# Attention products of two key tiles in one run of every second filled step, ten exponential buffers, eight GLU row buffers

## The chip, the cores and the metric

One core of one Trainium2 chip. The metric is device time in microseconds of one execution: the kernel before took 2319.98 us, the median of three runs (2316.81 to 2325.04).

## The reference

Two layers, each an attention block and a GLU block, over 2048 rows of 448 numbers. Both blocks normalise their input (layer norm without weights) and add their result to it. Both layers use the same weights.

```python
q = (x @ wq)   # 16 heads of 28
k = x @ wk     # one head, shared by all 16
v = x @ wv
p = softmax(q k^T * 28 ** -0.5)
x = x + (p v) @ wo
h = sigmoid(x @ w_gate) * (x @ w_up)     # 1792 columns
x = x + h @ w_down
```

## The kernel before

The schedule is written by hand: the order in which the Python code issues instructions is the order of each engine's queue. Each projection uses fp16 operands split into a high and a low part.

Attention runs per layer in 256 steps (lines 1100 to 1131): 16 query tiles `u` of 128 rows, and in each 16 key tiles `kt` of 128 keys. A string, `ORDER`, lists what a step issues, letter by letter:

- `S`: `scores` (line 598). One matmul of a key tile with the queries of four heads into a bank `s`, then ScalarE's exponential into a tile `P` of 128 x 512 (L604). Four per step, one for each group of four heads.
- `P`: `pv` (line 607), the attention product of the step before: four fp32 matmuls (L612), each of 32 columns of the array, side by side, accumulated over the 16 key tiles in the bank `pv`. Each is issued as two instructions, so a product is eight instructions: two passes of four. After the last key tile ScalarE copies the bank to `pvs` (L616).
- `M`: one part of the row maxima of a later query tile (`mx_gen`, line 570): four matmuls `mx`, each on 32 rows of the array, side by side, in four banks (L584), and four VectorE reductions of them (L588). The generator is ahead of the scores and runs out before the layer's steps do.
- `F`: `fill.slice` (line 936), a slice of queued matmuls of other work: the GLU of earlier row blocks (`gp`, `up` through `chain`, L402; `dn`, L802), the output projection (`wo`, L705), the next layer's queries. The slice's size follows from the work left and the steps left (`rate`), shared over the `F` of a step. It also issues what was deferred for the other engines.
- `X`: bookkeeping of the side work (`tick`), loads and preparation.

`s`, `mx` and all fill banks come from one ring of seven banks (tag `f`, `NBK`); a bank is taken again when its reader is done. `pv` has an eighth bank of its own. The tiles `P` come from a ring of eight buffers (tag `P`, line 603), which at the start also holds four input tiles and an index tile (lines 80, 81).

GLU work of a layer begins when its first block of two row tiles is ready (`BLK[l, 0].fed == TB`). `ORDERS` (line 1084) has one string for the steps before and one for those after, both the same here; the choice is made at the start of a step, before `X` in which a block becomes ready. I call steps after it filled. A GLU block makes seven tiles `h` of 128 x 2 x 512 in fp16 (line 769), then its down products read them. `h` has `HB` = 9 buffers. At the start the same buffers stage 42 pieces of the weights (line 248), whose squares are summed on TensorE (L144) to find scales. The start is ordered by a small list scheduler (`Plan`, line 868) with assumed costs; `HB` limits how many pieces it loads ahead (line 1073).

```python
1084  ORDERS = ["XFSFSFSFSPM", "XFSFSFSFSPM"]
1103  ORDER = ORDERS[(l, 0) in BLK and BLK[l, 0].fed == TB]
1110  elif o == "P":
1111      if prevP is not None:
1112          pv(*prevP)
1130  fill.slice(rate / ORDER.count("F"))
1131  prevP = (l, u, kt, P)
```

Of the kernel before, what the change touches and what calls it, by code (L numbers as in the profile page):

```python
# [8 lines left out]
F32 = mybir.dt.float32  # L9
F16 = mybir.dt.float16  # L10
BF16 = mybir.dt.bfloat16
I32 = mybir.dt.int32
# [8 lines left out]
def interleaved_layers_kernel(ctx: ExitStack, tc: tile.TileContext, x, wq, wk, wv, wo, wg, wu, wd, out, layers=2):  # L21
# [7 lines left out]
    _, S, D = x.shape  # L29
# [1 line left out]
    H, Dh = 16, 28  # L31
    NT, NB, G, KT, FC = S // 128, S // 512, H // 4, S // 128, F // 128
    U = NT
    TB, WB, HB, PF = 2, 4, 9, [4]
    NBL = NT // TB
    RQE, LD = nc.scalar, (0, 1, 2, 3)
    X0, X1, X2, X3, X4 = 3.0, 0.75, 5.0, 11.0, 17.0
# [10 lines left out]
    wk1 = ctx.enter_context(tc.tile_pool(name="wk1", bufs=2))  # L48
# [14 lines left out]
    xr0 = {}  # L63

    def load_x0(i, n, buf, eng=nc.sync):
        v = buf.rearrange("p n -> p () n") if n == 1 else buf
        eng.dma_start(v, x[0, i * 128:(i + n) * 128].rearrange("(t p) n -> p t n", p=128))
        for t in range(n):
            xr0[i + t] = v[:, t]
# [7 lines left out]
    load_x0(8, 2, wk1.tile([128, 2, D], F32, tag="XT2", name="xr0"))  # L77
    load_x0(10, 2, wk1.tile([128, 2, D], F32, tag="XT2", name="xr0"))
    for i in range(12, NT):
        load_x0(i, 1, wk1.tile([128, D], F32, tag="P", name="xr0", bufs=8))  # L80
    jp = wk1.tile([128, 128], I32, tag="P", name="jp", bufs=8)
    nc.gpsimd.iota(jp, pattern=[[1, 128]], base=0, channel_multiplier=-1)
    id16 = cst.tile([128, 128], F16, name="id16")
    nc.vector.tensor_scalar(id16, jp, 0.0, None, op0=OP.is_equal)
# [21 lines left out]
    def flush(every=False):  # L106
        todo, pend[:] = pend[:], []
        for i, (due, fn) in enumerate(todo):
            if due > now[0] and not every:
                pend.append((due, fn))  # L110
            else:
                fn()
        if every and pend:
            flush(True)
# [219 lines left out]
    def paced(step):  # L334

        k = next((i for i in range(len(PLAN) - 1) if PLAN[i + 1][0] > step), None)
        if k is None:
            n = 10 ** 6
        else:
            (a, p), (b, q) = PLAN[k], PLAN[k + 1]  # L340
            n = p + (q - p) * (step + 1 - a) / (b - a)
        while prepd[0] < n and ready[0] < 2 + FC:
            next(prep[0])
            prepd[0] += 1
# [76 lines left out]
    def layer_tiles(l):  # L421
        KK[l] = lay.tile([128, 2, S], F16, tag="KK", name="KK")
        VV[l] = lay.tile([128, KT, 32], F32, tag="VV", name="VV")
        nc.vector.memset(VV[l][:, :, 28:32], 0.0)
        nc.vector.memset(VV[l][:, :, 28:29], 1.0)
# [93 lines left out]
    def parts_of(l, u):  # L519

        ends = KEYS[l > 0 and u == 0]
        return list(zip(ends, ends[1:]))
# [11 lines left out]
    def load_qh(l, u):  # L534
        b, t = divmod(u, 4)
        if l + b == 0:
            QH[l, u] = QH0[:, :, t * 128:(t + 1) * 128]
            return
        assert QDONE[l, b] == G
        q = wk1.tile([128, G, 128], F16, name="QH", bufs=2)  # L540
        QH[l, u] = q
        nc.sync.dma_start(q, qd[l % 2][b, :, 0, :, t * 128:(t + 1) * 128].rearrange("g p n -> p g n"))
# [6 lines left out]
    def mx_ready(l, n):  # L549

        keys = parts_of(l, 0)
        return KVD[l] * 128 >= keys[n // G][1] if n < G * len(keys) else True
# [45 lines left out]
    def scores(l, u, kt, g, P):  # L598
        assert ("m", l, u) in stored, (l, u, kt)
        s = psf.tile([128, 512], F32, tag=BANKS["s"], name="s", bufs=NBK[BANKS["s"]])  # L600
        nc.tensor.matmul(s, KK[l][0:96, 0, kt * 128:(kt + 1) * 128], QS[l, u][:, g].rearrange("p h n -> p (h n)"),  # L601
                         start=True, stop=True)
        p = wk1.tile([128, 512], F32, tag="P", name="P", bufs=8)
        nc.scalar.activation(p, s, AF.Exp, scale=esc)  # L604
        P.append(p)

    def pv(l, u, kt, P):
        if kt == 0:
            PVS[l, u] = psv.tile([128, 512], F32, tag="v", name="pv")
        v = PVS[l, u]  # L610
        for g in range(4):
            nc.tensor.matmul(v[32 * g:32 * g + 32], VV[l][:, kt], P[g], start=kt == 0, stop=kt == KT - 1,  # L612
                             tile_position=(0, 32 * g))
        if kt == KT - 1:
            o = wk1.tile([128, 512], F32, name="pvs", bufs=1)
            nc.scalar.copy(o, v)  # L616
            PVS[l, u] = o


    XTQ, BLK = {}, {}  # L620
    side, held = [], set()

    def later(*stages):

        side.append([stages[0][0], list(stages)])

    def tick():

        for s in list(side):
            s[0] -= 1  # L630
            if s[1][0][1].__name__ in ("fd", "db") and held:
                s[0] = max(s[0], 1)
            if s[0] <= 0:
                flush()
                fill.run(s[1].pop(0)[1]())
                if s[1]:
                    s[0] = s[1][0][0]
                else:
                    side.remove(s)
# [441 lines left out]
    xr0 = None  # L1081

    early[0] = False
    ORDERS = ["XFSFSFSFSPM", "XFSFSFSFSPM"]
    MORE = (5, 10)
    FIRST = KT * TB + 16
    KEEP = 28000
# [1 line left out]
    for l in range(layers):  # L1089
        mx = mxs[l]  # L1090
        final = l + 1 == layers
        if not final:
            layer_tiles(l + 1)
        fill.slice(QCH)
        flush(True)
        next(mx, None)
        fill.slice(QCH)
        prevP = None
        rate = 0.0
        for step in range(U * KT):  # L1100
            u, kt = divmod(step, KT)
            P = []
            ORDER = ORDERS[(l, 0) in BLK and BLK[l, 0].fed == TB]
            for o in ORDER:
                if o == "S":
                    scores(l, u, kt, len(P), P)
                elif o == "M":
                    for _ in range(1 + (u == 0 and kt in MORE)):
                        next(mx, None)
                elif o == "P":  # L1110
                    if prevP is not None:
                        pv(*prevP)
                elif o == "X":
                    if u == U - 1 and not final and (l + 1, 0) not in QH and QDONE.get((l + 1, 0)) == G:
                        load_qh(l + 1, 0)
                    if u and kt == 1:
                        b = (u - 1) // TB
                        if (l, b) not in BLK:
                            BLK[l, b] = Block(l, b)
                        later(*BLK[l, b].tile(u - 1))  # L1120
                    if l == 0:
                        paced(step)
                    tick()
                    fed = sum(BLK[l, b].fed == TB for b in range(NBL) if (l, b) in BLK)
                    if fed < NBL - 1:
                        rate = fill.left / max(FIRST + TB * KT * fed - step, 1)
                    else:
                        rate = max(fill.left - KEEP, 0) / (U * KT - step)
                else:
                    fill.slice(rate / ORDER.count("F"))  # L1130
            prevP = (l, u, kt, P)
        pv(*prevP)
        flush(True)
        later(*BLK[l, NBL - 1].tile(U - 1))
        if not final:
            mxs[l + 1] = mx_gen(l + 1)
        n = done = 0
        last = G * len(parts_of(l + 1, 0))
        while side or pend or fill.urgent or (fill.gens if final else done < last):
            tick()  # L1140
            for _ in range(4):
                fill.slice(VS / 4)
            n += 1
            if not final and done < last and QDONE.get((l + 1, 0)) == G and mx_ready(l + 1, done):
                if n >= 3 or done >= last - G:
                    next(mxs[l + 1])
                    done += 1
                    n = 0
# [21 lines left out]
```

## Time and profile before

| | us |
|---|---|
| median of three runs | 2319.98 |
| profiled execution, own time | 2324.69 |
| its span, first to last instruction | 2322.9 |
| TensorE matmul busy | 2239.4 |
| VectorE busy | 1633.2 |
| ScalarE busy | 1549.8 |

The granted TensorE clock averages 0.99 of full speed. Times in rows are microseconds from the span's start unless marked ns; PE is TensorE, PEld its weight loads, DVE VectorE, ACT ScalarE. `out<-in` are the program's names, x is the number of instructions merged in a row. The end of a matmul is modelled and includes its way through the array, so successive matmuls overlap in a row's times; the distance from one start to the next is what TensorE spent. In square brackets stands how long the engine sat idle before, and what released it.

### The profile page before, as it was taken

What the parts mean: (1) busy time and instruction counts of PE and PEld (TensorE: products, weight loads), DVE (VectorE), ACT (ScalarE), POOL (GpSimd) and SP (SyncE); (2) the same over time, 40 slices, a digit from 0 to 9 for tenths busy, and PEclk for the clock granted to TensorE, in tenths of its full rate; (3) what the DMA queues carried; (4) which work ended last, traced back from release to release, by engine and by line L of the source; (5) the groups of instructions that cost most, each with busy time, mean ns of one, the idle gap of its engine ahead of it and who ended that gap; (6) DMA issues with size and microseconds to landing.
All of it is one profiled execution on the core that took longest, in us unless ns stands there. A gap on an engine that the chain in (4) does not pass through costs nothing.

```text
span 2322.9 us, 41223 instructions
## 1 busy us (share of the span) xinstructions
PE 2239.4 (96%) x15854; PEld 1007.0 (43%) x15854; DVE 1633.2 (70%) x2911; ACT 1549.8 (67%) x2498; POOL 322.3 (14%) x553
## 2 busy tenths in 40 slices
PE   6988899999999999999999999999999999999999
PEld 3422144444444444444563224444353444444456
DVE  6688887777677777774366988777777777777322
ACT  4277776777667677777513887767676767777741
POOL 4315661001010000101002000000000000000010
PEclk9999999999999999999999999999999999999999
DMA  9514562423323132333342012232231313232233
GB/s 236 155 30 125 150 199 59 110 59 95 108 60 100 59 110 59 114 75 87 105 139 84 19 41 78 77 103 77 76 92 50 107 59 100 59 112 66 85 103 122
DMA packets 225894, 217.55 MB, mean 94 GB/s; under 512 B 155488, under 2 KB 189216, under 8 KB 225696
## 3 DMA queue, kind: packets, MB, share of 16 engines
q1 hardware_dynamic: 219760, 199.19, 30.1%
q0 software_dynamic: 4256, 14.68, 1.8%
q8 instruction: 124, 2.03, 0.4%
q10 hardware_dynamic: 1680, 1.03, 0.2%
q14 instruction: 74, 0.61, 0.1%
HBM read 175.37 MB, written 23.59 MB: 86 GB/s over the span
## 4 chain that ended last, share of the span: by engine, by line
PE 84%; DVE 9%; DMA 3%; SPq 1%; ACT 1%; POOL 1%; issue 1%; ACTq 0%; DVEq 0%; POOLq 0%
PE pv L612 19%; PE s L601 17%; PE gp L402 12%; PE up L402 12%; PE dn L802 11%; DVE mp L588 7%; PE mx L584 6%; PE wo L705 3%; PE qp L402 2%; ACT P L604 1%; DMA XT<-hl 1%; DMA wgu<-wgu_d 1%; SPq L531 1%; DMA xr<-in_A_x_dram 0%; POOL hl L1047 0%
## 5 line engine op out<-in xcount | busy, mean ns | idle before, releaser
L604 ACT ACTIVATE P<-s,esc 128x512 f32<-128x512 f32 x2048 | 1326.5, 689 | 501.3 <-PE s L601 472.4
L588 DVE TENSOR_REDUCE mp<-mx 128x1 f32<-128x512 f32 (+1 forms) x2064 | 1269.8, 678 | 443.2 <-PE mx L584 442.0
L601 PE MATMUL s<-QS,KK 96*128 96x512 f16 x2048 | 749.7, 384 | 31.4 <-DVE mp L588 15.7
L402 PEld LDWEIGHTS <-wgu 128*128 128x128 f16 x4928 | 458.5, 97 | 224.1 <-issue 81.3
L612 PE MATMUL pv<-P,VV 128*32 128x512 f32 x4096 | 551.8, 611 | 0.9 <-ACT pvs L616 0.9
L402 PE MATMUL gp<-XT,wgu 128*128 128x256 f16 x2464 | 368.0, 273 | 3.1 <-DMA wgu<-wgu_d 2.8
L402 PE MATMUL up<-XT,wgu 128*128 128x256 f16 x2464 | 369.1, 272 | 0.0
L802 PE MATMUL dn<-WD,h 128*128 128x448 f16 x1344 | 316.8, 353 | 0.0
L601 PEld LDWEIGHTS <-KK 96*128 96x128 f16 x2048 | 190.8, 97 | 157.9 <-issue 80.7
L584 PEld LDWEIGHTS <-QH 32*128 32x128 f16 x2064 | 54.3, 91 | 429.5 <-issue 428.4
L584 PE MATMUL mx<-KK,QH 32*128 32x512 f16 (+1 forms) x2064 | 220.4, 385 | 10.9 <-ACT P L604 4.9
L802 PEld LDWEIGHTS <-h 128*128 128x128 f16 x1344 | 123.6, 97 | 135.1 <-issue 21.5
L612 PEld LDWEIGHTS pv<-P,VV 128*32 128x32 f32 x4096 | 81.4, 108 | 216.3 <-issue 205.1
L688 POOL TENSOR_TENSOR lb<-pvs,lb 128x512 f32<-128x512 f32 x32 | 41.0, 1280 | 871.8 <-DMA lb<-sums 756.2
L773 DVE SCALAR_TENSOR_TENSOR th<-th,up 128x512 f32<-128x512 f32 x112 | 76.1, 679 | 66.5 <-PE up L402 61.6
L360 POOL TENSOR_SCALAR rs<-mv 128x1 f32<-128x1 f32 x48 | 10.9, 227 | 737.3 <-DVE mv L355 737.3
L765 ACT ACTIVATE th<-gp,gsc 128x512 f32<-128x512 f32 x112 | 76.7, 685 | 45.2 <-PE gp L402 45.2
L777 DVE SCALAR_TENSOR_TENSOR h<-th,h 128x512 f16<-128x512 f32 x112 | 76.7, 685 | 40.8 <-ACT h L776 40.6
L776 ACT ACTIVATE h<-th 128x512 f16<-128x512 f32 x112 | 69.7, 622 | 48.9 <-DVE th L773 48.9
L705 PE MATMUL wo<-WO,oT 128*128 128x448 f16 x384 | 94.2, 356 | 0.0
L402 PE MATMUL qp<-XT,WQ 128*128 128x512 f16 x352 | 86.1, 386 | 0.0
L488 ACT ACTIVATE qst<-qp 128x512 f16<-128x512 f32 x28 | 16.7, 597 | 61.9 <-PE qp L402 36.4
(135 smaller groups left out, 798.1 us busy)
## 6 DMA issues: line engine op xcount, KB each, us to landing
wgu<-wgu_d SPq DMA_DIRECT2D x224, 512.0 KB
QS<-qd SPq DMA_DIRECT2D x384, 32.0 KB
lb<-sums SPq DMA_DIRECT2D x128, 64.0 KB
qd<-qst POOLq DMA_DIRECT2D x28, 256.0 KB, 2.8
wgu_d<-sgu POOLq DMA_DIRECT2D x14, 512.0 KB, 3.6
xr<-in_A_x_dram SPq DMA_DIRECT2D x24, 224.0 KB
QH<-qd SPq DMA_DIRECT2D x28, 128.0 KB
x2d<-x SPq DMA_DIRECT2D x16, 224.0 KB
```

The lines of the kernel that those rows point to most:

```text
L402: nc.tensor.matmul(ps, a, b, start=n == 0, stop=n == 10)
L584: nc.tensor.matmul(ps[h][:, :k1 - k0], qh[32 * h:32 * h + 32, g], KK[l][32 * h:32 * h + 32, 1, k0:k1], start=True, stop=True, tile_positio ...
L588: nc.vector.tensor_reduce(mp[:, g, h, kb:kb + 1], ps[h][:, :k1 - k0], axis=AX.X, op=OP.max)
L601: nc.tensor.matmul(s, KK[l][0:96, 0, kt * 128:(kt + 1) * 128], QS[l, u][:, g].rearrange("p h n -> p (h n)"), start=True, stop=True)
L604: nc.scalar.activation(p, s, AF.Exp, scale=esc)
L612: nc.tensor.matmul(v[32 * g:32 * g + 32], VV[l][:, kt], P[g], start=kt == 0, stop=kt == KT - 1, tile_position=(0, 32 * g))
L705: nc.tensor.matmul(p, v["oT"][:, a, h * 128:(h + 1) * 128], WO[:, c, h], start=n == 0, stop=n == 11)
L765: defer(lambda: nc.scalar.activation(th, gp.rearrange("p j n -> p (j n)"), AF.Tanh, scale=gsc))
L773: nc.vector.scalar_tensor_tensor(t, th, 1.0, up.rearrange("p j n -> p (j n)"), op0=OP.add, op1=OP.mult)
L776: nc.scalar.activation(h[:, 0], t, AF.Copy, scale=2.0 ** -17)
L777: defer(lambda: nc.vector.scalar_tensor_tensor(h[:, 1], t, 2.0 ** -17, h[:, 0], op0=OP.mult, op1=OP.subtract), 1)
L802: nc.tensor.matmul(p, hs[f // 2][:, a, o:o + 128], WD[:, f, c], start=n == 0, stop=n == 3 * FC - 1)
```

## The change

In filled steps the order now alternates. Even steps issue two score slices, then the products of the two steps before, one behind the other, then the maxima and two more score slices. Odd steps issue no product, and the maxima stand between the third and the fourth score. Products wait in a list, `ready_p`; before the filled steps it holds one entry, and the order is the old one. After the last step the list is emptied. `P` has ten buffers instead of eight (2 KB a partition each), `h` eight instead of nine (2 KB each). `PF` was not used.

```diff
-    TB, WB, HB, PF = 2, 4, 9, [4]
+    TB, WB, HB, PB = 2, 4, 8, 10
...
-        load_x0(i, 1, wk1.tile([128, D], F32, tag="P", name="xr0", bufs=8))
-    jp = wk1.tile([128, 128], I32, tag="P", name="jp", bufs=8)
+        load_x0(i, 1, wk1.tile([128, D], F32, tag="P", name="xr0", bufs=PB))
+    jp = wk1.tile([128, 128], I32, tag="P", name="jp", bufs=PB)
...
-        p = wk1.tile([128, 512], F32, tag="P", name="P", bufs=8)
+        p = wk1.tile([128, 512], F32, tag="P", name="P", bufs=PB)
...
-    ORDERS = ["XFSFSFSFSPM", "XFSFSFSFSPM"]
+    ORDERS = ["XFSFSFSFSPM"] * 2, ["XFSFSPPMFSFS", "XFSFSFSMFS"]
...
-        prevP = None
+        ready_p = []
...
-            ORDER = ORDERS[(l, 0) in BLK and BLK[l, 0].fed == TB]
+            ORDER = ORDERS[(l, 0) in BLK and BLK[l, 0].fed == TB][step % 2]
...
-                    if prevP is not None:
-                        pv(*prevP)
+                    if ready_p:
+                        pv(*ready_p.pop(0))
...
-            prevP = (l, u, kt, P)
-        pv(*prevP)
+            ready_p.append((l, u, kt, P))
+        for a in ready_p:
+            pv(*a)
```

## Rows read from the trace of the kernel before

**Rows 1.** The page, busy time of each engine: us, share of span, instructions.

```profile
PE 2239.4 (96%) x15854; PEld 1007.0 (43%) x15854; DVE 1633.2 (70%) x2911; ACT 1549.8 (67%) x2498; POOL 322.3 (14%) x553
```

**Rows 2.** The page, the chain that ended last, by engine.

```profile
PE 84%; DVE 9%; DMA 3%; SPq 1%; ACT 1%; POOL 1%; issue 1%; ACTq 0%; DVEq 0%; POOLq 0%
```

**Rows 3.** Waits of PE, 288 to 1133 us: us in total, times, longest us.

```profile
PE s L601 <- DVE mp L588: 3.8, 13, 0.9
PE s L601 <- ACT P L604: 1.8, 2, 1.4
```

**Rows 4.** Waits of PE, 1413 to 2240 us.

```profile
PE s L601 <- DVE mp L588: 3.4, 15, 0.2
```

**Rows 5.** Timeline of PE, 1010.5 to 1016.6: start, duration, instruction.

```profile
1011.66 0.40 PE L584 MATMUL mx<-KK,QH 32*128 32x512 f16 x4
...
1013.09 0.38 PE L601 MATMUL s<-QS,KK 96*128 96x512 f16 x1
...
1013.75 0.38 PE L601 MATMUL s<-QS,KK 96*128 96x512 f16 x1
1013.97 0.60 PE L402 MATMUL up<-XT,wgu 128*128 128x256 f16 x4
1014.40 0.38 PE L601 MATMUL s<-QS,KK 96*128 96x512 f16 x1
1014.72 1.06 PE L612 MATMUL pv<-P,VV 128*32 128x512 f32 x8
1015.71 0.39 PE L584 MATMUL mx<-KK,QH 32*128 32x512 f16 x4
1016.04 0.61 PE L402 MATMUL up<-XT,wgu 128*128 128x256 f16 x4
1016.49 0.38 PE L601 MATMUL s<-QS,KK 96*128 96x512 f16 x1
```

**Rows 6.** Timeline of PE at 1015.4, inside that product: its second pass.

```profile
1015.17 0.61 PE L612 MATMUL pv<-P,VV 128*32 128x512 f32 x4
```

**Rows 7.** Timeline of PE, 1004.5 to 1005.2.

```profile
1004.62 0.38 PE L601 MATMUL s<-QS,KK 96*128 96x512 f16 x1
1004.93 0.22 PE L564 MATMUL mt<-id,m 128*16 128x128 f16 x1
```

**Rows 8.** Timeline of PEld, 1013.9 to 1016.5: the weight loads of that product.

```profile
1014.71 0.16 PEld L612 LDWEIGHTS pv<-P,VV 128*32 128x32 f32 x8 [0.32 <-issue]
```

**Rows 9.** Scores in three stretches: count, ns (min/median/max), first and last start us.

```profile
L601 PE MATMUL s<-QS,KK x208: 376/377/634, 109.6 to 286.7; 96*128 96x512 f16 x104
...
L601 PE MATMUL s<-QS,KK x740: 376/381/390, 1413.6 to 2166.5; 96*128 96x512 f16 x185
...
L601 PE MATMUL s<-QS,KK x76: 379/381/391, 2168.6 to 2235.7; 96*128 96x512 f16 x76
```

**Rows 10.** Timeline, 944.7 to 956: a score in a step without fills.

```profile
949.64 0.38 PE L601 MATMUL s<-QS,KK 96*128 96x512 f16 x1 [0.23 <-DVE mp L588]
```

**Rows 11.** Timeline of PE, 1079 to 1086: the first layer's last steps, without `mx`.

```profile
1082.59 1.06 PE L612 MATMUL pv<-P,VV 128*32 128x512 f32 x8 [0.43 <-ACT pvs L616]
1083.58 0.61 PE L402 MATMUL gp<-XT,wgu 128*128 128x256 f16 x4
```

**Rows 12.** Timeline of all engines, 1000 to 1016: VectorE and ScalarE in filled steps.

```profile
1010.32 0.68 DVE L773 SCALAR_TENSOR_TENSOR th<-th,up 128x512 f32<-128x512 f32 x1
...
1012.08 2.48 DVE L588 TENSOR_REDUCE mp<-mx 128x1 f32<-128x512 f32 x4 [1.08 <-PE mx L584]
...
1012.43 0.38 PE L601 MATMUL s<-QS,KK 96*128 96x512 f16 x1
...
1012.85 0.69 ACT L604 ACTIVATE P<-s,esc 128x512 f32<-128x512 f32 x1 [0.88 <-PE s L601]
```

**Rows 13.** Timeline of PE, 0 to 112 us: squares of weight pieces, four instructions each.

```profile
94.27 1.22 PE L144 MATMUL sqs<-rmax 128*112 128x112 bf16 x20 [0.23 <-DVE mp L588]
...
101.26 1.19 PE L144 MATMUL sqs<-rmax 128*112 128x112 bf16 x8 [0.71 <-DMA rmax<-in_B_w_down_dram]
```

## The prediction

> **What bounds the kernel now.** I read the page's busy shares first: TensorE is busy 96% of the span [rows 1]. Overlapped matmuls could make that share a mere appearance, so the chain of waits comes next: 84% of the chain that ended last is TensorE's, VectorE has 9%, ScalarE 1% [rows 2]. Then the waits of TensorE alone, over the stretch in which the first layer has fill work (288 to 1133 us): its longest totals are 3.8 us for VectorE's row maxima and 1.8 us for the exponentials; in the second layer 3.4 us [rows 3, 4]. So in a filled step no other engine holds TensorE up: a step lasts as long as its own stream. What is to be found is time inside that stream in which it does no work.
>
> The timeline of two filled steps shows it [rows 5]. From `mx` to `mx` a step takes 4.05 us (1011.66 to 1015.71). A score followed by fills occupies 0.22 us until the next matmul starts (1013.75 to 1013.97), but 0.32 us when a product `pv` follows (1014.40 to 1014.72). The product needs 0.99 us until `mx` starts, and `mx` 0.33 us until the fills run on (1015.71 to 1016.04). The product is two passes of four matmuls side by side. The second pass starts 0.45 us after the first (1014.72, and 1015.17 in [rows 6]), but `mx` starts 0.54 us after the second. So a pass followed by one of its own kind costs 0.09 us less than one followed by another shape. A change of shape drains the array: after a score 0.10 us, after a product 0.09 us, after `mx` 0.11 us, three changes a step.
>
> **The change, part by part.**
>
> *The order of a filled step.* Before, each step goes score, product, maxima, fill: three changes of shape, six in a pair. Afterwards the even step has score, product, product, maxima, fill, and the odd one score, maxima, fill: five. The four fills, four scores and one `mx` of a step remain. Before, a pair spends 2 x (0.32 + 0.99 + 0.33) = 3.28 us from its last score before a change of shape to the fills behind. Afterwards the even step takes 0.32 + 0.90 + 0.99 + 0.33, where 0.90 is two passes followed by passes of their own kind. The odd step takes a score followed by `mx`, and 0.33. The trace has no such neighbours in a filled step; the nearest is a score followed by the small transpose `mt`, also another shape: 0.31 us (1004.62 to 1004.93) [rows 7]. That is the value I take. Its lower bound is 0.22, a score with no change of shape, its upper 0.33, what `mx` itself takes before fills. Sum 3.18 us, **0.10 us less in a pair**; hundredths of the rows make that 0.09 to 0.10, and I count 0.09, the one drain that goes.
>
> The boundary between the two products is the other unknown. Below it is 0.44 (twice the 0.22 of a 512-column score, as a pass streams twice the columns), above it is 0.54, the drain. I take 0.45, because the first and second pass are the same shape on the same accumulator, and the row of weight loads shows all eight loads of a product issued within 0.16 us, those of the second pass included, while the first streams [rows 8].
>
> The Trainium skill, page "TensorE: Matmul & The Clock Gate", Part 3, "The mechanism", says of tiled matmuls that a weight load overlaps running matmuls only where its row group differs, though it also allows loads into a background buffer. All products use the same rows, so by the strict reading the second would start only after a drain, the boundary would be 0.54, and the pair would gain nothing. The row of weight loads speaks against that reading: the second pass's loads use the same rows as the matmuls then running.
>
> *How many pairs.* 208 scores (52 steps) stand before the first layer's fills [rows 9]. In the second layer 740 scores (185 steps) lie between the first filled step and the last one with `mx`, then 76 (19 steps) without [rows 9]; 52 + 185 + 19 = 256, and the first layer has the same shape. The new order starts one step after the first fills. So 92 pairs per layer have `mx`, 184 in all, and 19 in all have not. Where a score waits for VectorE's maxima, as at 949.64 [rows 10], the step has no fills and VectorE sets it; 13 + 15 such waits [rows 3, 4], about two to a step, take 14 pairs out. 170 x 0.09 = 15.3 us.
>
> *Steps without `mx`.* There the product lies between a score and fills, 0.99 us too (1082.59 to 1083.58) [rows 11]. Two steps now cost 2 x (0.32 + 0.99) = 2.62, afterwards 0.32 + 0.90 + 0.99 + 0.22 = 2.43: 0.19 us less, 19 x 0.19 = 3.6 us. The first product of a query tile waited 0.43 us for the copy of the one before [rows 11]. Products now come two steps after that copy, so this goes in both layers: 0.9 us. Together **19.8 us** gained.
>
> *Exponentials, ten buffers instead of eight.* At the second product the tiles of two steps and two of the present one are alive, ten. The third exponential needs the first product's release, which stands ahead of its score on TensorE, so nothing is queued behind a wait. The second product needs the odd step's last exponential. That score starts 2 x 0.66 us (two fill-and-score intervals, from 1013.09 to 1013.75 and its like), 0.32 us and one product of 0.90 us before it: 2.54 us. The exponential starts 0.42 us after its score (1012.43 to 1012.85) and takes 0.69 us [rows 12]: 1.11 us, 1.43 us to spare, two more ScalarE passes of that size. Cost nothing while that cover holds.
>
> *The spacing of the maxima.* They were 4.05 us apart. Now the odd `mx` comes 0.33 + 0.45 (to the first score) + 4 x 0.66 + 0.31 = 3.73 us after the even one, and the even one 0.33 + 0.45 + 2 x 0.66 + 0.32 + 0.90 + 0.99 = 4.31 us after the odd. `mx` and scores share a ring of seven banks, so four new ones need the last maxima read: VectorE starts 0.42 us after `mx` and takes 2.48 us, 2.90 in all [rows 12]. 0.83 us remains, enough for one VectorE pass of 0.68 us, not for two. Bounds: nothing, or 0.53 us in one of eight pairs, 12 us. As `mx` hardly ever waits now [rows 3, 4], I take **2 us**.
>
> *Eight GLU row buffers instead of nine.* A block uses seven and its down products precede the next block's GLU on TensorE, so one spare still covers it. The same buffers stage 42 weight pieces at the start. There TensorE's last squares already wait 0.71 us for a load [rows 13]. A load waits for one piece later, 0.24 us in that run (1.22 us for five) [rows 13], up to 3 us where the hand-made planner spaces the squares wider; it may also choose another order, so minus 3 to plus 3. I take **1 us**.
>
> Sum: 19.8 - 2 - 1 = 16.8 us less. The profiled execution took 2324.69 us and becomes 2307.9. It lies 4.7 us above the median of the runs, 2319.98, from which the same sum gives **2303.2 us**.
>
> **The rivals.**
>
> *The second product drains or loads first* (chance 0.16). The boundary is 0.54, and the pair with `mx` gains nothing. The rows of the two passes speak against it; for it, both passes belong to one matmul, and across two matmuls of this shape I see nothing. Steps without `mx` still gain 0.10 x 19 = 1.9, the copy 0.9; with 3 us of costs 2320. The change would then keep the same number of drains: it does not do what its order says. The strict reading of the Trainium skill, "TensorE: Matmul & The Clock Gate", Part 3, is this case.
>
> *VectorE's maxima come late, slower* (0.08). Place: the odd `mx`, and the seven-bank ring. A block's 32 steps have seven GLU tiles with two VectorE passes of 0.68 us each. If both run ahead of the maxima in the short interval, `mx` waits 2 x 0.68 - 0.83 = 0.53 us. In 7 pairs of 16 that is 80 x 0.53 = 42 us: 2303 - 2 + 42 = 2343. It decides from a mean wait of 0.11 us per pair on. Against it: the long interval gives back 1.41 us to VectorE, and one pass usually stands between two groups.
>
> *A score followed by `mx` costs no drain* (0.06): 0.09 us more per pair, 2287. The small transpose speaks against it.
>
> **How the numbers follow.** My forecast has 0.70: its own range 2296 (no waits, all 184 pairs, a start 3 us better) to 2314 (12 us of waits). For 8 in 10 the range must take in the draining rival, so it ends at 2321; the slower rival, and the cheaper score, stay outside. A measurement of this kernel tells some 0.3%, 7 us, from no change. The forecast lies 16.8 us off, so nearly all of its share (0.66) and the cheap score count as faster, 0.72; the rest of it and most of the draining rival as the same, 0.18; slower 0.10.
>
> **What the changed profile would show.** Right: in filled steps sixteen `pv` instructions in one row, `mx` 1.89 us after the first; `mx` to `mx` alternately near 3.7 and 4.3 us; a pair 0.09 us under the 8.1 of now; waits of TensorE for maxima still under 6 us a layer. Wrong: products 0.99 us apart (draining), `mx` rows with a VectorE releaser of half a microsecond (the ring), product rows waiting for exponentials (the cover of 1.43 us gone), or scores later than the 109.6 us at which they now begin [rows 9] by more than 3 us (the start).

## The result, and the profile after

The changed kernel is slower: 2330.02 us (median of four runs) against 2318.39 for the kernel before (four runs), a ratio of 1.0045 with a 95% interval of 1.0026 to 1.0064. I had forecast 16.8 us less and a range that ended at 2321. The profiled execution took 2328.52 us, its span is 2326.7.

The page, busy shares and the chain that ended last:

```profile
PE 2238.4 (96%) x15854; PEld 1036.3 (45%) x15854; DVE 1636.5 (70%) x2911; ACT 1535.4 (66%) x2498; POOL 324.4 (14%) x553
...
PE 79%; DVE 11%; ACT 4%; DMA 3%; issue 1%; SPq 1%; POOL 1%; ACTq 0%; DVEq 0%; POOLq 0%
```

TensorE has as many instructions as before [rows 1]. In the chain it gave up five points, and ScalarE went from 1% [rows 2] to 4%. The timeline of the changed kernel, 893 to 912 us, shows a pair of filled steps, from the maxima of one odd step to those of the next. Left out are VectorE, the weight loads, all fills but two, and some scores and exponentials:

```profile
893.49 0.38 PE L601 MATMUL s<-QS,KK 96*128 96x512 f16 x1
893.80 0.39 PE L584 MATMUL mx<-KK,QH 32*128 32x512 f16 x4
894.12 0.28 PE L402 MATMUL up<-XT,wgu 128*128 128x256 f16 x1
...
896.06 0.38 PE L601 MATMUL s<-QS,KK 96*128 96x512 f16 x1
896.37 1.92 PE L612 MATMUL pv<-P,VV 128*32 128x512 f32 x16
...
898.23 0.40 PE L584 MATMUL mx<-KK,QH 32*128 32x512 f16 x4
...
899.48 0.69 ACT L604 ACTIVATE P<-s,esc 128x512 f32<-128x512 f32 x1 [2.25 <-PE s L601]
...
900.07 0.62 ACT L776 ACTIVATE h<-th 128x512 f16<-128x512 f32 x1
...
900.32 0.38 PE L601 MATMUL s<-QS,KK 96*128 96x512 f16 x1
...
900.59 0.68 ACT L604 ACTIVATE P<-s,esc 128x512 f32<-128x512 f32 x1
...
901.16 0.69 ACT L765 ACTIVATE th<-gp,gsc 128x512 f32<-128x512 f32 x1
...
901.63 0.38 PE L601 MATMUL s<-QS,KK 96*128 96x512 f16 x1
901.73 3.92 ACT L604 ACTIVATE P<-s,esc 128x512 f32<-128x512 f32 x6
901.95 0.90 PE L584 MATMUL mx<-KK,QH 32*128 32x512 f16 x4
...
902.78 0.61 PE L402 MATMUL up<-XT,wgu 128*128 128x256 f16 x4
```

The drains went as reckoned. A score with the maxima behind it takes 0.31 us (893.49 to 893.80), as I took from [rows 7]. The two products take 1.86 us until `mx` (896.37 to 898.23), where one took 0.99 [rows 5]; I had 1.89. What is new stands in the last rows. The odd step's `mx` at 901.95 lasts 0.90 us where 0.39 is usual [rows 5], and the fills run on 0.83 us after its start instead of 0.33. Its four matmuls were pulled apart: a bank was still being read. Narrower windows of the same timeline show the third exponential and the fourth matmul by themselves:

```profile
901.73 0.69 ACT L604 ACTIVATE P<-s,esc 128x512 f32<-128x512 f32 x1
...
902.47 0.37 PE L584 MATMUL mx<-KK,QH 32*128 32x512 f16 x1
```

Three of the four had started at 901.95; the fourth started 0.05 us after that exponential ended. ScalarE had begun the exponential of the third score of its run only at 901.73, though that score began at 900.32, because the two passes of a GLU tile (900.07 and 901.16) lay in between. Before that run it had idled 2.25 us behind the products.

The page's list of waits hardly shows this, since matmuls of a group overlap in it. So I worked out the waits from the starts of all matmuls in the trace: the distance to the next start, less what the same neighbours take when nothing holds them, where the rest is over 0.04 us. Each is put down to the engine whose read of a bank ended 0.04 to 0.07 us before the late start. The stages run from score to score; the steps named are numbered from 0 in a layer.

| us | before | changed |
|---|---|---|
| first layer, steps 53 to 236 (filled, with `mx`) | 773.7 | 782.3 |
| - waits for ScalarE's reads | 3.6 | 14.6 |
| - waits for VectorE's reads | 14.4 | 18.2 |
| second layer, the same steps | 751.3 | 750.2 |
| - waits for ScalarE's reads | 0.0 | 12.9 |
| - waits for VectorE's reads | 7.9 | 6.0 |
| both layers, steps 237 to 255 and what follows | 352.4 | 347.3 |

In both layers together ScalarE's waits rose from 3.6 to 27.5 us. That eats the drains that were saved. Of the 27.5 us, some 20 lie inside the groups of maxima; about half of these end with an exponential's read of a score's bank, the other half with ScalarE's first GLU pass (L765), which reads the bank `gp`. The second layer comes out 1.1 us better, the first 8.6 worse. The layers differ in the clock. The stretches where TensorE was granted half of it (1.2 GHz) in the first layer's filled steps, in the view by stretches (columns: PE, PEld, DVE, ACT and POOL busy, PEclk, DMA share, GB/s), and the first layer's fill stage of before:

```profile
547.70:551.10 3.40, 3.40 (x12) 1.49 (x11) 3.26 (x6) 1.82 (x3) 0.14 (x1) 0.50 0.96 262
674.00:677.40 3.40, 3.40 (x10) 1.38 (x11) 2.52 (x6) 0.69 (x1) 1.41 (x3) 0.51 0.32 93
827.60:831.00 3.40, 3.40 (x16) 1.63 (x19) 3.00 (x6) 1.75 (x4) 0.00 (x0) 0.51 0.92 244
960.70:964.10 3.40, 3.40 (x16) 1.67 (x19) 3.13 (x6) 1.70 (x4) 0.01 (x1) 0.50 0.96 254
```

```profile
288.00:1140.00 852.00, 841.75 (x6127) 387.49 (x6124) 602.15 (x1062) 612.65 (x986) 114.80 (x224) 1.00 0.33 93
```

Counting half the work at half the clock, the four cost an estimated 6.8 us, most of the 9.7 us that set the first layer apart from the second. Ahead of each, TensorE had stood still for a while. Two of them, in the timeline of the changed kernel:

```profile
673.96 0.27 PE L564 MATMUL mt<-id,m 128*16 128x128 f16 x1 [1.95 <-DVE m L559]
674.16 1.30 PE L802 MATMUL dn<-WD,h 128*128 128x448 f16 x3
```

```profile
826.04 0.59 PE L601 MATMUL s<-QS,KK 96*128 96x512 f16 x2 [0.96 <-DVE mp L588]
...
827.94 1.06 PE L402 MATMUL gp<-XT,wgu 128*128 128x256 f16 x4
```

At 674 the transpose of the row maxima waited 1.95 us for VectorE's pass in front of it (L559), and the three `dn` behind it took 1.30 us, where 0.74 is usual. At 826 it is a step without fills: with no product in the odd step, a score waits 0.96 us for VectorE (0.23 before, [rows 10]), and the fills behind run at half speed, 1.06 us against 0.61. The stretches at 547.70 and 960.70 followed steps like that one too (gaps of 0.96 us at 546.41 and 959.27). But not every such gap had a stretch behind it: the changed kernel's at 414.71 (0.96 us) had none, nor had two of before (1.36 us at 309.99, 0.97 at 600.30). What decides between them these traces do not show.

### The profile page after: what moved, and what is told of

The parts are those of the page before. It is cut to its first block, busy times and chain, and to the rows that moved or that the text cites. A ratio compares the mean times of both kernels' runs of the same rounds, so it can differ in the third digit from the quotient of the medians.

```text
span 2326.7 us, 41280 instructions
## 1 busy us (share of the span) xinstructions
PE 2238.4 (96%) x15854; PEld 1036.3 (45%) x15854; DVE 1636.5 (70%) x2911; ACT 1535.4 (66%) x2498; POOL 324.4 (14%) x553
## 4 chain that ended last, share of the span: by engine, by line
PE 79%; DVE 11%; ACT 4%; DMA 3%; issue 1%; SPq 1%; POOL 1%; ACTq 0%; DVEq 0%; POOLq 0%
PE pv L612 18%; PE s L601 15%; PE dn L802 11%; PE up L402 11%; PE gp L402 10%; DVE mp L588 8%; PE mx L584 6%; PE wo L705 3%; PE qp L402 3%; ACT P L604 3%; ACT th L765 1%; DMA wgu<-wgu_d 1%; SPq L531 1%; DMA XT<-hl 1%; DMA rgu<-in_B_w_gate_dram 0%
## 5 line engine op out<-in xcount | busy, mean ns | idle before, releaser
L612 PE MATMUL pv<-P,VV 128*32 128x512 f32 x4096 | 514.3, 609 | 0.0
L584 PE MATMUL mx<-KK,QH 32*128 32x512 f16 (+1 forms) x2064 | 240.6, 386 | 16.8 <-ACT P L604 5.8
L612 PEld LDWEIGHTS pv<-P,VV 128*32 128x32 f32 x4096 | 103.0, 109 | 260.6 <-issue 249.7
L773 DVE SCALAR_TENSOR_TENSOR th<-th,up 128x512 f32<-128x512 f32 x112 | 76.2, 680 | 66.3 <-PE up L402 49.9
L777 DVE SCALAR_TENSOR_TENSOR h<-th,h 128x512 f16<-128x512 f32 x112 | 79.6, 710 | 46.6 <-ACT h L776 46.5
L765 ACT ACTIVATE th<-gp,gsc 128x512 f32<-128x512 f32 x112 | 77.0, 687 | 49.8 <-PE gp L402 49.8
L776 ACT ACTIVATE h<-th 128x512 f16<-128x512 f32 x112 | 69.7, 623 | 48.8 <-DVE th L773 48.8
```

The source lines that it names most:

```text
L584: nc.tensor.matmul(ps[h][:, :k1 - k0], qh[32 * h:32 * h + 32, g], KK[l][32 * h:32 * h + 32, 1, k0:k1], start=True, stop=True, tile_positio ...
L765: defer(lambda: nc.scalar.activation(th, gp.rearrange("p j n -> p (j n)"), AF.Tanh, scale=gsc))
L773: nc.vector.scalar_tensor_tensor(t, th, 1.0, up.rearrange("p j n -> p (j n)"), op0=OP.add, op1=OP.mult)
L776: nc.scalar.activation(h[:, 0], t, AF.Copy, scale=2.0 ** -17)
L777: defer(lambda: nc.vector.scalar_tensor_tensor(h[:, 1], t, 2.0 ** -17, h[:, 0], op0=OP.mult, op1=OP.subtract), 1)
```

## The experiments

Theory A: the odd step's maxima and the scores around it wait for banks that ScalarE frees late. Rival V: VectorE's reductions come late, as my slower case had it. Rival B: the ninth GLU buffer is missed. Rival D: the late transposes are the cause. Ratios are to the kernel before on the same chip.

**Eight GLU buffers alone.** The kernel before with `HB` changed, nothing else.

```diff
-    TB, WB, HB, PF = 2, 4, 9, [4]
+    TB, WB, HB, PF = 2, 4, 8, [4]
```

> The kernel before with eight GLU row buffers instead of nine, nothing else. Theory A (the odd step's maxima wait for banks that ScalarE frees late): this part is innocent, 2318 to 2322 us, ratio to before within 0.999 to 1.002; the first score starts at about 110.5 us instead of 109.6, as it does after the change. Rival B (the buffer that was taken away costs the time, at the start or where a GLU block begins): most of the 10 us show here, 2326 to 2331 us.

Measured 2319.58 us, before 2319.51; ratio 1.000 (0.9991 to 1.001). Stage by stage it is the kernel before (773.6 and 751.3 us in the filled steps with `mx`). Its first score came at 108.1 us, not at 110.5, so a start later by an us or two is no matter of this buffer. Rival B is out, as far as the old order shows it; nine buffers with the new order were not run.

**A fill ahead of the odd step's maxima.**

```diff
-    ORDERS = ["XFSFSFSFSPM"] * 2, ["XFSFSPPMFSFS", "XFSFSFSMFS"]
+    ORDERS = ["XFSFSFSFSPM"] * 2, ["XFSFSPPMFSFS", "XFSFSFSFMS"]
```

> The changed kernel with the odd step's order score, fill, score, fill, score, fill, maxima, score: one fill slice stands between the third score and the maxima, which come about 0.35 us later after that score; same number of drains. In the changed kernel the four matmuls of a group of maxima, which start within 0.01 us when nothing holds them, are pulled apart by 26 us in all over the filled steps. Theory A: they are held by the banks of the scores just before, so 0.35 us more lets ScalarE finish; the 26 us fall below 10, the time to 2308 to 2316 us, under that of before. Rival B (buffers) or rival C (the order costs the time elsewhere, for example by the late transposes of the row maxima): nothing changes, 2326 to 2332 us.

Measured 2332.99 us, ratio 1.0057 (1.0045 to 1.007): no gain, and a miss for A as I had put it. The pulling apart did fall, from 28 to 13 us, but ScalarE's waits did not, from 27.5 to 33.7 us. They moved to the score now right behind the maxima, as the page's waits of TensorE show (us in total, times, longest):

```profile
PE s L601 <- ACT P L604: 15.7, 58, 0.7
```

In the changed kernel that row has 6.7 us in 22 waits. By its time alone the run suits rivals B and C; the waits keep A. So it is not the place of the maxima alone. Eight scores stand in a run without a product, and with ScalarE behind, the ring's banks hold TensorE up at one place or the next.

**Maxima earlier in the odd step.**

```diff
-    ORDERS = ["XFSFSFSFSPM"] * 2, ["XFSFSPPMFSFS", "XFSFSFSMFS"]
+    ORDERS = ["XFSFSFSFSPM"] * 2, ["XFSFSPPMFSFS", "XFSFSMFSFS"]
```

> The changed kernel with the odd step's maxima after its second score instead of its third, so 3.1 us after the even step's maxima instead of 3.7. Theory A (ScalarE): the fourth bank is still that of the score four back with no product between, so the pulling apart stays, 15 to 30 us, and the time between 2318 and 2332 us. Rival V (VectorE's reductions, 2.9 us with their start, are late, as the slower case of the prediction has it): 0.2 us are left where 0.8 us were, so each VectorE pass of 0.68 us in that interval is a wait of 0.5 us; the 26 us become 45 or more and the time 2345 us or more.

Measured 2346.49 us, ratio 1.0119 (1.0102 to 1.0136). VectorE's waits went from 24.2 to 54.0 us, ScalarE's from 27.5 to 23.1. The size is V's, but the reads are mostly others than V names. In the timeline of this kernel, TensorE's rows first (the third from a narrow window inside the second), then VectorE's:

```profile
1488.30 0.40 PE L584 MATMUL mx<-KK,QH 32*128 32x512 f16 x4
1491.57 0.65 PE L584 MATMUL mx<-KK,QH 32*128 32x512 f16 x4
...
1491.85 0.37 PE L584 MATMUL mx<-KK,QH 32*128 32x512 f16 x1
...
1488.72 2.48 DVE L588 TENSOR_REDUCE mp<-mx 128x1 f32<-128x512 f32 x4 [2.75 <-PE mx L584]
1491.12 0.68 DVE L773 SCALAR_TENSOR_TENSOR th<-th,up 128x512 f32<-128x512 f32 x1
```

3.27 us behind the last group, `mx` is pulled apart to 0.65. The reductions of that group had ended at 1491.20, before `mx` began; its fourth matmul started at 1491.85, 0.05 us after VectorE's GLU pass (L773, to 1491.80), which reads the bank `up`. By the starts of matmuls, some 16 us of the maxima's waits here end with that pass, 11 with VectorE's read of `wo` (L710), and some 11 with reductions. So VectorE does become the limit at the shorter distance, through the banks of the fills more than through its reductions. In the change the distance is 3.72 us (898.23 to 901.95), and VectorE's waits hardly grew: V is not the limit there.

**The high part of the GLU tile on GpSimd.**

```diff
-                        nc.scalar.activation(h[:, 0], t, AF.Copy, scale=2.0 ** -17)
+                        if f < FC - 2:
+                            nc.gpsimd.tensor_scalar(h[:, 0], t, 2.0 ** -17, None, op0=OP.mult)
+                        else:
+                            nc.scalar.activation(h[:, 0], t, AF.Copy, scale=2.0 ** -17)
```

> The changed kernel with the high part of six of the seven GLU tiles of a block written by GpSimd instead of ScalarE: one of ScalarE's two GLU passes (0.62 us each) is gone from the run of scores, VectorE has the same work. Theory A: ScalarE is what holds the banks, so the 26 us fall by about half, and the time to 2312 to 2320 us. Rival V (VectorE): the 26 us stay, 2326 to 2334 us.

Measured 2351.7 us, ratio 1.0139 (1.0121 to 1.0156). ScalarE's waits fell from 27.5 to 15.7 us, as A says, but VectorE's rose from 24.2 to 49.3: scores waited up to 2.6 us for reductions. VectorE's second GLU pass (L777 in the change) needs that high part. GpSimd takes 1.50 us for it, ScalarE 0.62; VectorE waits for it, and reductions queue behind. As a test of the time it decides nothing.

**Transposes kept to their date.** Each holds its due slice when all that is deferred is flushed ahead of the last down product.

```diff
-                if f == FC - 1:
-                    flush(True)
+                if f == FC - 1:
+                    flush(True, True)
...
-        defer(fin, LAG)
+        defer(fin, LAG, True)
...
-            if due > now[0] and not every:
+            if due > now[0] and (not every or hold and timed):
```

> The changed kernel, where the flush ahead of the last down product no longer brings the transpose of the row maxima forward. In the changed kernel's first layer one such transpose stood right behind the reductions that it needs and TensorE waited 2.0 us, after which its clock ran at half rate for 3.4 us. Theory A (banks held for ScalarE's reads cost most, this is one accident): 3 to 5 us less than the changed kernel, 2324 to 2328 us, ratio to before 1.002 to 1.004; the half-rate stretch at 674 us is gone, the others stay. Rival D (the late transposes are the cause): back to 2319 us or under.

Measured 2322.4 us, ratio 1.0011 (0.9997 to 1.0025). The stretch at half clock behind the transpose is gone, three others stand. The first layer's filled steps take 780.0 us instead of 782.3, the second's 750.2 as before, and ScalarE's waits stay at 28.4 us. By the median the gain is 6 to 8 us, more than the 3 to 5 that I gave it, but the ten runs lie between 2315.63 and 2331.08, and the interval reaches rival D's 2319. The trace speaks against D: of the 6.2 us by which its span is shorter than the changed kernel's, 5.0 lie ahead of step 53, where the edit does nothing, and only 2.3 in the first layer's filled steps.

**ScalarE's second GLU pass in the pause.** Same work on every engine; the pass L776 is issued behind the second score of an even step.

```diff
-                    defer(parts, 4)
+                    if paired[0]:
+                        late.append(parts)
+                    else:
+                        defer(parts, 4)
...
                 elif o == "P":
+                    in_pause()
                     if ready_p:
```

> The changed kernel with ScalarE's second pass of each GLU tile (L776, 0.62 us) issued only behind the second score of an even step, where two products and the maxima follow and ScalarE idles some 2 us. Same work on every engine, VectorE's orders but for that tile unchanged. Theory A: of the waits of scores and maxima that end with a read by ScalarE (12.9 us in the second layer's filled steps with maxima, 14.6 in the first's) about 40% go, 8 to 12 us in all, time 2318 to 2324 us. Rival V (VectorE) or D: 2328 to 2333 us, these waits unchanged.

Measured 2313.68 us, ratio 0.9971 (0.996 to 0.9983): faster than both kernels. ScalarE's waits fell from 27.5 to 16.1 us, by 41%, as A had it. VectorE's rose a little (28.1 us). The two filled stages lost 6.5 and 4.0 us (775.8 and 746.2), 10.5 in all, which is what A gave. The time fell by more: 16 us between the medians, 16.1 between the traces, and in these 6.3 lie ahead of step 53, which the edit does not touch and where the traces of this kernel and its variants with seven banks end anywhere from 287 to 294 us. Two stretches at half clock remain in the first layer. Part of its 6.5 us may be chance: the 1.95 us wait for the transpose is still there (667.02 us) with no stretch behind it. The second layer has none in either trace, and its 4.0 us are free of the clock. In its timeline, 880 to 902 us (lines of code are six further down here):

```profile
885.04 1.92 PE L618 MATMUL pv<-P,VV 128*32 128x512 f32 x16
...
886.00 0.63 ACT L782 ACTIVATE h<-th 128x512 f16<-128x512 f32 x1
...
888.15 1.28 ACT L610 ACTIVATE P<-s,esc 128x512 f32<-128x512 f32 x2 [1.52 <-PE s L607]
...
889.33 0.68 ACT L771 ACTIVATE th<-gp,gsc 128x512 f32<-128x512 f32 x1
...
889.90 3.97 ACT L610 ACTIVATE P<-s,esc 128x512 f32<-128x512 f32 x6
...
890.61 0.40 PE L590 MATMUL mx<-KK,QH 32*128 32x512 f16 x4
```

The pass lies beside the products, where ScalarE had been idle; only the `th` pass is left in the run of scores, and `mx` takes its 0.40 us.

**One bank less, before and after.** `NBK["f"]` from 7 to 6 in both kernels.

```diff
-    NBK = {"f": 7, "s": 2, "m": 3}
+    NBK = {"f": 6, "s": 2, "m": 3}
```

> The kernel before with a ring of six banks instead of seven. Theory A: a product stands ahead of each group of maxima, so one bank less costs waits of VectorE above all, in the steps without fills and some in the filled ones: 2330 to 2370 us. It is the base for the next run.

> The changed kernel with a ring of six banks. Theory A: the changed order needs the banks more, since the odd step's maxima take those of the scores just before: the gap to the kernel before with six banks grows from 11 us with seven to 30 us or more. Rival (the ring has no part in it: the order costs its time through the clock, the transposes or the reductions): the gap stays between 5 and 20 us.

Measured 2427.84 us for the kernel before (ratio 1.047) and 2448.43 for the changed one (1.0555). The base is far over what I had expected: of some 110 us between the traces, 68 lie in the filled steps with `mx` and 44 ahead of those steps. The gap is 20.6 us where it was 9 to 12: it grew, but less than the 30 that I gave A and hardly over the rival's 20, so the times don't decide. The stages and the waits do. The changed order is 11 us longer in the filled steps with `mx` of each layer, 22 in all, where seven banks gave 8.6 and -1.1; there ScalarE's waits rise from 11.1 us in the old order to 81.3 in the new one, while VectorE's fall from 83.7 to 59.0. The new order leans on ScalarE and the ring, and gives part of that back elsewhere.

**The changed kernel again, and repairs together.** The first is the changed kernel itself; the second has the edits of the transposes and of the pause; the third the transposes and another order; the fourth that order with both.

```diff
-    ORDERS = ["XFSFSFSFSPM"] * 2, ["XFSFSPPMFSFS", "XFSFSFSMFS"]
+    ORDERS = ["XFSFSFSFSPM"] * 2, ["XSSPPMFSFSF", "XFSFSFMFSFS"]
```

> The changed kernel once more, beside the next three on one chip, as their base: 2326 to 2332 us, ratio to before 1.003 to 1.006. Its filled steps of the first layer again hold three or more stretches at half clock, the kernel before none.

> The changed kernel with both repairs: ScalarE's second GLU pass behind the second score of the even step, and the transposes of the row maxima kept to their date. Theory A with the accident added: the two gains add, 16 us and 4 us, 2308 to 2313 us, ratio to before 0.994 to 0.998. If they share a cause: 2313 to 2318 us.

> The changed kernel with transposes kept to their date and another order: the even step has score, score, product, product, maxima, fill, score, fill, score, fill, the odd one score behind fill three times, the third fill ahead of the maxima, then two more fills each with a score. Two of the scores now stand directly ahead of the products, where ScalarE has time to read them, and the maxima follow a fill. Theory A: ScalarE's waits at the maxima halve, 2310 to 2320 us. Rival: the second product now waits for exponentials instead, or scores for maxima, 2325 us or more.

> The order of the run before this one and ScalarE's second GLU pass behind the second score of the even step. Theory A: 2303 to 2312 us, the least of all. Rival: no better than the order of the change with the same two repairs, 2308 to 2315 us, as the second product waits for ScalarE, which has one pass more there.

| | us | ratio (95%) | waits for ScalarE, VectorE |
|---|---|---|---|
| changed again | 2328.34 | 1.0038 (1.0024 to 1.0053) | 28.3, 24.6 |
| pause and date | 2313.29 | 0.9975 (0.9965 to 0.9985) | 15.3, 25.6 |
| scores before products, date | 2336.35 | 1.007 (1.0057 to 1.0083) | 20.3, 38.8 |
| the same with the pause | 2324.01 | 1.0019 (1.0008 to 1.0029) | 13.7, 36.6 |

The changed kernel repeats its time and its waits, with five stretches at half clock in the first layer's filled steps. By the medians the two repairs don't add: 2313.29 is the pause alone within its interval. In the trace the first layer's filled steps do shrink further (770.8 us against 775.8), but that execution, 2310.06, is the fastest of nine and has one stretch at half clock there instead of two. The other order is a miss, as its rival had it: it lessens ScalarE's waits, but scores standing close behind the maxima run into their banks, and VectorE's waits grow by 12 to 14 us. There too the pause is worth 12 us, though 2324.01 lies over both ranges that I gave.

## Why the prediction was wrong

**What bounds the kernel: right.** TensorE's stream set the filled steps, and VectorE, ScalarE and the loads were nearly hidden. But [rows 3] and [rows 4] gave 3.8 and 3.4 us of waits for VectorE, where the starts of matmuls show 14.4 and 7.9: the rows leave out what is hidden in overlapping matmuls.

**The drains: right, and too small.** One drain fewer per pair, at the places named. Without waits and clock the filled steps with `mx` lost some 12.5 us per layer: in the first 8.6 us more came out with 21 us of added loss (ScalarE 11.0, VectorE 3.8, half clock and small gaps 6.3), in the second 1.1 less with 11.5. That is 0.136 us per pair of 92, where I counted 0.09: the two products take 1.86 us, not 1.89, and the remaining 0.01 to 0.02 is within the hundredths of the rows. The draining rival, in which the second product waits for the first to empty, is refuted. The steps without `mx` gave 5.1 us with the tail; I had 4.5.

**Eight buffers: right in kind.** I gave 1 us, the run alone shows none.

**The spacing of the maxima: the step that failed.** I wrote that "four new ones need the last maxima read" and reckoned VectorE's 2.90 us against 3.73. Both are right, and VectorE's waits rose by only 1.9 us. But some banks of the odd `mx` had last held scores or the GLU's `gp`, and the reader of both is ScalarE. Before, each group stood behind a product, 1 us in which ScalarE could catch up; now the odd group stands in a run of eight scores. I did weigh ScalarE's lag, but for the second product alone, with 1.43 us to spare. There it holds: no product waits for an exponential. Against the banks that the odd maxima take I never held it, and took 2 us with an upper bound of 12; ScalarE alone added 24. The bound counted the wrong reader.

**The clock: missing.** I let waits cost their own length. Four gaps of 1 to 2 us in the first layer were followed by a stretch at half clock that cost an estimated 1.7 us each; a fifth was not. The 0.72 that I gave to faster rested on a bound that took in neither these stretches nor ScalarE's reads.

The sum, from these: 25 us of drains and 5 us without `mx` gained; 24 us for ScalarE, 2 for VectorE, 7 for clock and gaps lost. That gives 3 us more, and the profiled spans differ by 3.8. The medians differ by 9 to 12: the profiled run of before lay 5 us over its median, and other runs of the changed kernel show a mean clock down to 0.983, where most of before lie at 0.99. Which gaps those were is not in a trace, so the 5 to 8 us between the spans and the medians stay open. So does why the repaired transposes gain 6 to 8 us by the medians alone, but 2.3 in their trace's filled steps and nothing by the medians with the pause.

## What to carry to other kernels

When work is gathered into longer runs, list for every buffer of a shared ring who reads it last in the new order: the engine that lagged unseen behind a pause may now hold the ring. A pause that one engine makes is room for another: moving 0.62 us of ScalarE's work into it took 10.5 us from the filled steps, and a median 9 to 12 us over the kernel before became one 7 us under it. And a new wait of a microsecond on TensorE can cost more than its length: behind four of five here the clock fell to half.

## What the runs showed of the hardware

A product directly behind another of the same shape starts 0.43 us after the last pass of the one ahead, about twice the 0.22 us of a score, where a change of shape takes 0.54 [rows 5, 6]. In the changed kernel, 662 to 679 us, the loads of the later passes stand beside the running ones:

```profile
668.67 0.16 PEld L612 LDWEIGHTS pv<-P,VV 128*32 128x32 f32 x8 [0.40 <-issue]
668.68 1.92 PE L612 MATMUL pv<-P,VV 128*32 128x512 f32 x16
...
669.13 0.13 PEld L612 LDWEIGHTS pv<-P,VV 128*32 128x32 f32 x4 [0.30 <-issue]
669.56 0.13 PEld L612 LDWEIGHTS pv<-P,VV 128*32 128x32 f32 x4 [0.30 <-issue]
...
670.53 0.10 PEld L584 LDWEIGHTS <-QH 32*128 32x128 f16 x4 [0.84 <-issue]
```

The loads at 669.13 and 669.56 are 0.46 and 0.43 us after those ahead, and the matmuls' passes start 0.45, 0.43 and 0.43 us apart, without the 0.09 us of a drain. The strict reading of the Trainium skill ("TensorE: Matmul & The Clock Gate", Part 3, "The mechanism"), that a weight load waits where the row group is the same, does not hold here; its remark on a background buffer fits.

A ring of six banks instead of seven cost the old order 107 us (2427.84 against 2320.55, 4.7%), more than any order tried here.

Some waits of 0.96 us and more on TensorE were followed by 3.4 us at half the granted clock (0.50 to 0.51), and others of the same length were not: in the first layer's filled steps four of five in the changed kernel, none of two in the kernel before.
